# Half-height matmul operands outside the scores made full-height in a fused attention and mixer kernel

## The chip, the cores and the metric

The kernel runs on one core of a Trainium2 chip. The metric is the device time of one execution in microseconds. TensorE is PE in the rows, its weight loads PEld, VectorE DVE, ScalarE ACT, GpSimd POOL, and SP issues the DMAs.

## The reference

Causal attention of 4 batches x 12 heads (448 positions, 64 wide), then two MLP-mixer blocks on the [4, 448, 768] result. All is float32 or wider; the weights come in as doubles.

```python
attn = softmax(mask(q @ k.T / 8)); x = (attn @ v) as [4, 448, 768]
u = x + (relu(x.T @ w_tok1) @ w_tok2).T          # 448 -> 256 -> 448
x2 = u + relu(u @ w_ch1) @ w_ch2                 # 768 -> 1536 -> 768
g, v = split(relu(x2 @ w_in))                    # 512 each
v_n = (v - mean) / sqrt(var + 1e-6)
v_s = w_spatial @ v_n + b_spatial                # over the 448 positions
out = (g * v_s) @ w_out
```

## The kernel before

Every matrix product runs on operands that are split into two parts, hi and lo, and is the sum of hi x hi, hi x lo and lo x hi: three matmuls where one would do. The 448 positions are cut into chunks of 64, 128, 128 and 128, so that the causal mask wastes little. The first chunk has only 64 rows, half the height of the 128 x 128 array, and what the kernel does with those 64 rows is what the change is about. There are five places.

The scores (`scores`, line 190) multiply over the 64 channels of a head, one head on the upper half of the partitions and one on the lower half. The change leaves them as they are.

The other four:

- **The value's first chunk** (`weighted`, line 269, V0 and V1 in the order for the two heads of a pair): 64 keys of head j stand on the half `r` of the partitions, and the product with the transposed probabilities takes that half alone, twice (hi and lo of the probabilities). Then lines 271, 273 and 275 multiply the other three key chunks at full height. All accumulate into one PSUM bank.
- **The transposes** (`transposed`, line 247, T0 in the order): for the first key chunk of both heads there are four transposes, one for each query chunk. The query chunk of 64 rows is a half-height transpose, 64 x 64; the other three are 128 x 128.
- **The token mixing** (`token_mix`, lines 329 to 331 and 121 to 123, tile `psm<-xs,wt`): the hidden layer of a group of three pairs of heads is made in two parts, h0 and h1. Each is eleven matmuls: line 329, then line 330, which takes the low weights of the first chunk on the upper half of the partitions alone, then nine at full height. There are eight groups, so line 330 runs 16 times.
- **The spatial product** of the second block (`spatial`, lines 623 to 625, tile `psp`): the same shape again, with line 624 the half-height one; four column blocks for each of four batches, so 16 times.

The attention and the token mixing run interleaved, in an order that is written out by hand (`ORDER`): for each pair of heads a list of steps S (scores and softmax of a query chunk), T (transposes and their split), V, m (token mixing), q and v (splits of the inputs), each lagging the pair by up to three. Each engine takes its instructions in that order. There are 24 pairs. After that come the channel mixing (four batches x 12 weight chunks), the gated unit's input, the spatial products and the output projection.

POOL splits v into hi (line 76) and lo (line 82, tile `vhl`), splits the low part of q and k (line 82, tile `qk`), and multiplies the probabilities by the reciprocal sums (line 226). DVE does the row maxima (line 205), the low parts out of PSUM (lines 82 and 89), the sums into `U` (lines 280 and 364) and, in spare places, the narrowing of the doubles (lines 106, 108 and 110, tile `w`). ACT does the exponentials (line 217) and the high parts (line 74, and line 351 for `hid`).

Of the kernel before, what the change touches and what calls it, by code (L numbers as in the profile page):

```python
# [8 lines left out]
F32 = mybir.dt.float32  # L9
# [19 lines left out]
# The engines' order of work in the attention and token mixing, for one pair of heads: each name  # L29
# stands for the next step of a unit, each ' for one pair earlier.  # L30
# [9 lines left out]
def mixer_kernel(ctx: ExitStack, tc: tile.TileContext, qkv, wtok, w12, winu, winv, wsp, wout, bsp, out):  # L40
    """Every matrix product runs as float32r products of operands that are split
    exactly into two parts of 12 significant bits: hi * hi + hi * lo + lo * hi.

    On-chip memory is one pool of tagged slots which the phases share:
      U0-3     x^T, u^T, x2^T of each batch, later the gate
      G0-16    6 KB each: attention's and the token mixing's tiles, the 12 weight
               chunks of the channel mixing and the split of the running one, the
               input weights and normalised values of the gated unit
      X0-5     split operands of 448 columns, both parts
      h0-1     split hidden activations and gated values  # L50
      p0-1     narrow probabilities, unsplit gated values
      dbl0-1   float64 weights on their way in
    """
# [41 lines left out]
    def fetch(x):  # L95
        """Rows of doubles to SBUF as 32-bit words, the low word of each first."""
        n = 2 * x.shape[-1]
        t = slot(f"dbl{turn('dbl', 2)}", [2 * 2 * DM], U32, "dbl")
        nc.sync.dma_start(t[:, :n], x.bitcast(U32))
        return t[:, :n].rearrange("p (c t) -> p c t", t=2)  # L100

    def narrow_steps(w, d):
        """Doubles as words to float32: sign and top exponent bit, then the next 27 bits, then the top 3 of the low word."""
        w = w.bitcast(U32)
        lo, hi = d[:, :, 0], d[:, :, 1]
        nc.vector.tensor_scalar(w, hi, 3, 0x3FFFFFFF, op0=ALU.logical_shift_left, op1=ALU.bitwise_and)
        yield
        nc.vector.scalar_tensor_tensor(w, hi, 0xC0000000, w, op0=ALU.bitwise_and, op1=ALU.bitwise_or)  # L108
        yield
        nc.vector.scalar_tensor_tensor(w, lo, 29, w, op0=ALU.logical_shift_right, op1=ALU.bitwise_or)  # L110
        yield
# [5 lines left out]
    def mm3(ps, terms, first=True, last=True):  # L117
        """ps += sum of a.T @ b over terms of split operands (ah, al, bh, bl)."""
        n = len(terms)
        for i, (ah, al, bh, bl) in enumerate(terms):  # L120
            nc.tensor.matmul(ps, ah, bh, start=(first and i == 0), stop=False)  # L121
            nc.tensor.matmul(ps, ah, bl, start=False, stop=False)  # L122
            nc.tensor.matmul(ps, al, bh, start=False, stop=(last and i == n - 1))  # L123

# [15 lines left out]
    stage = [slot(f"G{i}", [3 * S], F32, f"stage{i}") for i in range(2)]  # L140
# [9 lines left out]
    def split_qk(n):  # L150
        """Splits q and k of a pair of heads."""
        st = stage[n % 2][:, : 2 * S]
        h, l = (slot(f"X{3 * (n % 2) + i}", [2 * S], F32R, "qk") for i in range(2))
        operands[n] = [h, l]
        parts = [slice(i * S, i * S + S) for i in range(2)]
        for c in parts:
            hi_part(h[:, c], st[:, c])
            yield
        for c in parts:
            lo_part(l[:, c], st[:, c], h[:, c], "dve" if n == 0 else "pool")  # L160
            if c is parts[1]:
                load_qk(n + 2)
            yield

    def split_v(n):
        """Splits v of a pair of heads, its parts side by side."""
        st = stage[n % 2][:, 2 * S :]
        vhl = slot(f"X{3 * (n % 2) + 2}", [7, 128], F32R, "vhl")
        v = st.rearrange("p (c d) -> p c d", d=64)
        hi_part(vhl[:, :, 0:64], v, "pool")  # L170
        yield
        lo_part(vhl[:, :, 64:128], v, vhl[:, :, 0:64], "pool")
        operands[n].append(vhl)
        load_v(n + 2)
        yield

    def scores(n, i):
        """Normalised probabilities of query chunk i; head 0 has its key chunks in reverse."""
# [20 lines left out]
        if i < 2 and "small" not in p:  # L199
            p["small"] = slot(f"p{n % 2}", [512], F32, "P10")  # L200
            p[1] = p["small"][:, 0:384].rearrange("p (j w) -> p j w", j=2)
            p[0] = p["small"][:, 384:512].rearrange("p (j w) -> p j w", j=2)
# [28 lines left out]
    def transposed(n, which, j):  # L231
        """Probabilities with keys on partitions, split: 0 for both heads' first key chunk, a and b of head j for the others."""
        P = [probs[n][i].rearrange("p j w -> p (j w)") for i in range(4)]

        def block(i, c):
            W, (k0, k1) = CHUNKS[i][1], CHUNKS[c]
            return P[i][:, slice(W + k0, W + k1) if j else slice(W - k1, W - k0)]

        if which == "0":
            blocks = [(q0, q1 - q0, P[i][: q1 - q0, q1 - 64 : q1 + 64]) for i, (q0, q1) in enumerate(CHUNKS)]  # L240
        elif which == "a":
            blocks = [(128 * (i - 1), 128, block(i, 1)) for i in (1, 2, 3)]
        else:
            blocks = [(128 * (i - 2), 128, block(i, 2)) for i in (2, 3)] + [(256, 128, block(3, 3))]
        ps = bank(SB + turn("t", TB), "pst")
        for o, M, src in blocks:
            nc.tensor.transpose(ps[:, o : o + M], src, ident[:M, :M])  # L247
        yield
        if which == "0":
            t = slot(f"h{n % 2}", [2, S], F32R, "T0")  # L250
        else:
            if (n, j) not in PT:
                PT[n, j] = slot(f"G{4 + j}", [4, 384], F32R, "Tab")
            t = PT[n, j][:, 0:2] if which == "a" else PT[n, j][:, 2:4]
        h, l = t[:, 0, :], t[:, 1, :]
        ps = ps[:, : h.shape[-1]]
        hi_part(h, ps)
        yield
        lo_part(l, ps, h)
        PT[n, which, j] = (h, l)  # L260
        yield

    def weighted(n, j):
        """x^T of head j: V^T P^T for V's two parts on the two halves of the partitions, then their sum."""
# [3 lines left out]
        for k in range(2):  # L268
            nc.tensor.matmul(ps[:, :S], vhl[r, 0, :], PT[n, "0", 0][k][r, :], start=(k == 0), stop=False)
        for k in range(2):  # L270
            nc.tensor.matmul(ps[:, 64:S], vhl[:, 1 + 3 * j, :], PT[n, "a", j][k], start=False, stop=False)  # L271
        for k in range(2):
            nc.tensor.matmul(ps[:, 192:S], vhl[:, 2 + 3 * j, :], PT[n, "b", j][k][:, 0:256], start=False, stop=False)
        for k in range(2):
            nc.tensor.matmul(ps[:, 320:S], vhl[:, 3 + 3 * j, :], PT[n, "b", j][k][:, 256:384], start=False, stop=(k == 1))
# [8 lines left out]
    WT = {}  # L284

    def load_tok():
        """Token weights, as steps."""
# [22 lines left out]
    def token_mix(n, m):  # L310
        """Part 3 * (n % 3) + m of 9 of the token mixing of a batch's three pairs of heads."""
# [6 lines left out]
        for s in todo:  # L318
# [7 lines left out]
            elif s[0] == "h":  # L326
# [3 lines left out]
                nc.tensor.matmul(p[:, :384], w[1][0:64, 0], x[0][0][0:64], start=False, stop=False)  # L330
# [42 lines left out]
    def split_slot(i, f):  # L373
        """For the split of part i of chunk f."""
        return f"G{15 + i}" if f % 2 == 0 else f"G{i}"

    def get_w12(f, nxt=True):
        """The weights' chunk f as float32, the next ones on their way."""
# [44 lines left out]
    WI = {}  # L423

    def get_win(i):
        """Input weights, part i of 4, split."""
# [92 lines left out]
    # the gate's columns, then the values, normalised over channels  # L519
# [14 lines left out]
    def value(lhs, key):  # L534
# [13 lines left out]
        # one Newton step of 1/sqrt(a)  # L548
# [44 lines left out]
    # spatial products, gating and the output weights  # L593
# [6 lines left out]
    def normed(b):  # L600
# [6 lines left out]
        ns.append((t[:, 0, :], t[o, 0, :]))  # L607
# [8 lines left out]
        return ns, o  # L616

    def spatial(b, ns, o):
        gs = []
        for f in range(NG):  # L620
            c = slice(128 * f, 128 * f + 128)
            ps = bank(turn("g", 4), "psp")[:, :S]
            nc.tensor.matmul(ps, ns[0][0][:, c], wsps[0][0], start=True, stop=False)
            nc.tensor.matmul(ps, ns[0][1][:, c], wsps[1][0][o], start=False, stop=False)
# [10 lines left out]
    def project(b, gs):  # L635
# [4 lines left out]
        # two row blocks wait for the last gated chunk together  # L640
# [20 lines left out]
    for b in range(B):  # L661
        gs = spatial(b, *ns)
# [6 lines left out]
def _layout(inputs):  # L669
    import numpy as np  # L670

    def chunked(a):
        """[448, n] -> [128, 4, n]: 64 rows (in both halves), then three times 128."""
# [7 lines left out]
    qkv = np.empty((B, NP, 128, 3 * S), q.dtype)  # L681
# [4 lines left out]
    qkv[..., 2 * S : 2 * S + D] = v[:, :, :64].reshape(B, NP, 128, D)  # L686
    qkv[..., 2 * S + D :] = (
# [45 lines left out]
```

## Time and profile before

| what | value |
|---|---|
| time, median of 3 runs | 898.4 us (896.5 to 899.64) |
| span of the profiled execution | 895.9 us |
| PE busy | 854.0 us (95%) |
| DVE, ACT, POOL busy | 510.1, 406.1, 423.8 us |
| attention and token mixing | from 0 to about 300 us |
| channel mixing, gated unit | about 300 to 785 us |
| spatial products and projection | 785 to 896 us |

The profiled execution has no time of its own beside the span from its first to its last instruction; the median of the runs is 2.5 us above it. Matmuls are pipelined, so their durations overlap, and the busy time of PE says little about how close it is to its limit. What one matmul takes from the next is read from the chain of work that ended last, where each piece counts only from the end of the piece before it.

### The profile page before, as it was taken

The numbers are of one execution on the slowest core, as the hardware profiler recorded it, in microseconds if no ns is written. First come the engines' busy times: TensorE is split into PE (matmuls) and PEld (weight loads), VectorE is DVE, ScalarE is ACT, GpSimd is POOL, SyncE is SP. The second block draws the span as 40 slices with busy tenths as digits, with TensorE's granted clock in tenths as the row PEclk, the third lists the DMA queues.
The fourth block names the chain that finished last, engine by engine and source line by source line (L and its number), as shares of the span: only waits on it lengthen the run. The fifth ranks groups of instructions, "written<-read, shape, count | busy, mean of one in ns | idle before, by whom it ended". The sixth has DMA issues, their size and how long they took to land.

```text
span 895.9 us, 12396 instructions
## 1 busy us (share of the span) xinstructions
PE 854.0 (95%) x4492; PEld 724.2 (81%) x4492; DVE 510.1 (57%) x1252; ACT 406.1 (45%) x958; POOL 423.8 (47%) x418
## 2 busy tenths in 40 slices
PE   4989999999999998999999999999989999999998
PEld 3667677677777887899999999999978888777877
DVE  5896998998889999240005000733382355364342
ACT  5686788788887322242224223433323133322111
POOL 5775776777776164545555544566640000322010
PEclk9988999999999999999999999999999999999999
DMA  5341323241210455200000000021101000001111
GB/s 191 116 150 53 133 65 124 67 137 48 76 31 11 142 212 209 74 0 1 1 1 1 1 1 1 15 99 70 64 20 58 1 1 1 1 20 42 62 62 62
DMA packets 13597, 54.24 MB, mean 61 GB/s; under 512 B 1504, under 2 KB 7776, under 8 KB 11104
## 3 DMA queue, kind: packets, MB, share of 16 engines
q1 hardware_dynamic: 13536, 53.45, 17.3%
q8 instruction: 35, 0.57, 0.3%
q14 instruction: 26, 0.21, 0.1%
HBM read 47.94 MB, written 5.51 MB: 60 GB/s over the span
## 4 chain that ended last, share of the span: by engine, by line
PE 73%; DVE 18%; ACT 5%; DMA 2%; issue 1%; POOL 0%; SPq 0%; ACTq 0%; DVEq 0%
PE acc L122 6%; PE acc L123 6%; PE acc L121 6%; PE ps L121 5%; PE ps L122 5%; PE ps L123 5%; PE pst L247 4%; PE pss L190 4%; DVE w L110 3%; DVE w L108 2%; PE psg L123 2%; PE psg L121 2%; PE psg L122 2%; PE pso L271 2%; ACT P L217 2%; PE psv L122 2%
## 5 line engine op out<-in xcount | busy, mean ns | idle before, releaser
L82 POOL TENSOR_TENSOR whl<-w,whl 128x768 fp32r<-128x768 f32 (+1 forms) x100 | 185.9, 1860 | 176.1 <-ACT whl L74 176.1
L89 DVE SCALAR_TENSOR_TENSOR hid<-ps,hid 128x448 fp32r<-128x448 f32 x48 | 29.7, 620 | 184.3 <-ACT hid L92 184.3
L74 ACT CAST whl<-w 128x768 fp32r<-128x768 f32 (+1 forms) x100 | 80.6, 806 | 114.1 <-PE acc L123 107.1
L226 POOL TENSOR_SCALAR P<-P,rs 128x320 f32<-128x320 f32 (+1 forms) x192 | 97.9, 523 | 66.9 <-DVE rs L223 57.3
L122 PE MATMUL acc<-hid,whl 128*128 128x448 f32 x288 | 106.3, 369 | 9.0 <-DVE hid L89 9.0
L123 PE MATMUL acc<-hid,whl 128*128 128x448 f32 x288 | 105.8, 367 | 0.0
L121 PE MATMUL acc<-hid,whl 128*128 128x448 f32 x288 | 105.8, 367 | 0.0
L121 PE MATMUL ps<-uhl,whl 128*128 128x448 f32 x288 | 105.4, 366 | 0.0
L122 PE MATMUL ps<-uhl,whl 128*128 128x448 f32 x288 | 105.4, 366 | 0.0
L123 PE MATMUL ps<-uhl,whl 128*128 128x448 f32 x288 | 105.2, 365 | 0.0
L217 ACT ACTIVATE P<-P,nm 128x320 f32<-128x320 f32 (+1 forms) x192 | 95.8, 503 | 6.6 <-DVE nm L205 6.5
L247 PE MATMUL pst<-ident,P 128*128 128x128 f32 (+1 forms) x384 | 72.9, 300 | 9.5 <-DVE rs L223 3.6
L190 PE MATMUL pss<-qk 64*128 64x448 f32 (+3 forms) x576 | 68.6, 344 | 9.6 <-ACT qk L74 5.5
L92 ACT ACTIVATE hid<-ps 128x448 fp32r<-128x448 f32 x48 | 26.1, 544 | 111.5 <-PE ps L123 111.4
L205 DVE CUSTOM_DVE_ANT_0 P<-pss,mask 128x320 f32<-128x320 f32 (+1 forms) x192 | 75.8, 410 | 1.2 <-PE pst L247 0.5
L190 PEld LDWEIGHTS pss<-qk 64*128 64x128 f32 (+1 forms) x576 | 43.7, 191 | 30.2 <-issue 15.5
L122 PEld LDWEIGHTS acc<-hid,whl 128*128 128x128 f32 x288 | 54.5, 189 | 15.2 <-DVE hid L89 10.9
L247 PEld LDWEIGHTS pst<-ident,P 128*128 128x128 f32 (+1 forms) x384 | 43.4, 148 | 25.9 <-issue 15.4
L121 PEld LDWEIGHTS acc<-hid,whl 128*128 128x128 f32 x288 | 54.5, 189 | 4.4
L123 PEld LDWEIGHTS acc<-hid,whl 128*128 128x128 f32 x288 | 54.5, 189 | 4.3
L123 PEld LDWEIGHTS ps<-uhl,whl 128*128 128x128 f32 x288 | 54.1, 188 | 4.3
L121 PEld LDWEIGHTS ps<-uhl,whl 128*128 128x128 f32 x288 | 54.1, 188 | 4.2
(144 smaller groups left out, 1872.1 us busy)
## 6 DMA issues: line engine op xcount, KB each, us to landing
dbl<-in_w SPq DMA_DIRECT2D x12, 1536.0 KB, 6.5
stage<-in_qkv SPq DMA_DIRECT2D x24, 448.0 KB, 3.3
stage<-in_qkv SPq DMA_DIRECT2D x24, 224.0 KB, 2.8
out_t<-out SPq DMA_DIRECT2D x24, 224.0 KB, 1.9
dbl<-in_winu SPq DMA_DIRECT2D x2, 1536.0 KB, 6.4
dbl<-in_winv SPq DMA_DIRECT2D x2, 1536.0 KB, 7.0
dbl<-in_wout SPq DMA_DIRECT2D x2, 1536.0 KB, 6.2
dbl<-in_wtok SPq DMA_DIRECT2D x1, 1024.0 KB, 7.3
```

What stands on the lines that cost most here:

```text
L74: nc.scalar.copy(hi, x)
L82: e.tensor_tensor(lo, x, hi.bitcast(F32), op=ALU.subtract)
L89: nc.vector.scalar_tensor_tensor(lo, x, 0.0, hi.bitcast(F32), op0=ALU.max, op1=ALU.subtract)
L110: nc.vector.scalar_tensor_tensor(w, lo, 29, w, op0=ALU.logical_shift_right, op1=ALU.bitwise_or)
L121: nc.tensor.matmul(ps, ah, bh, start=(first and i == 0), stop=False)
L122: nc.tensor.matmul(ps, ah, bl, start=False, stop=False)
L123: nc.tensor.matmul(ps, al, bh, start=False, stop=(last and i == n - 1))
L190: nc.tensor.matmul(pss[j][:M, :W], a[r, q0:q1], c[r, ks[j]], start=(k == 0), stop=(k == 2))
L205: nc.vector.tensor_tensor_reduce(out=P[:M, j, :], in0=pss[j][:M, :W], in1=mask[:M, S - 128 : S - 128 + W] if j == 0 or M == 64 else mask[: ...
L217: nc.scalar.activation(P[:M, j, :], P[:M, j, :], AF.Exp, bias=nm[:M, j : j + 1], scale=-1.0, accum_out=sums[:M, j : j + 1])
L226: nc.gpsimd.tensor_scalar(P[:M, j, :], P[:M, j, :], rs[:M, j : j + 1], 1.0, op0=ALU.mult, op1=ALU.mult)
L247: nc.tensor.transpose(ps[:, o : o + M], src, ident[:M, :M])
```

## The change

The half-height operands of the four places become full-height ones, so that outside the scores each matmul has 128 rows.

- Value: the split of v has 8 blocks of 64 columns instead of 7. Blocks 0 and 1 are the first key chunks of head 0 and head 1, each with zeros on the other head's half of the partitions. The zeros come in from memory with v: its load grows from 448 to 512 columns (224 to 256 KB a pair), and so do POOL's two splits of it.
- Transposes: the first query chunk is transposed as 128 x 128. Its rows 64 to 127 are zeros, set once by two memsets on POOL at the start, for which the two small tiles of probabilities are now allocated once and kept. The 64 columns too many are written over by the next transpose.
- Token mixing and spatial product: line 330 and line 624 take the low weights on both halves of the partitions, where the other operand holds hi on one half and lo on the other. So lo x lo comes in as well, in the same instruction.

No matmul is added or taken away, and none changes its place on its engine. The diff also takes out comments and docstrings; that part is left out here.

```diff
+    small = [slot(f"p{i}", [512], F32, f"P10{i}") for i in range(2)]
+    for t in small:
+        nc.gpsimd.memset(t[64:128, 384:512], 0.0)
-    stage = [slot(f"G{i}", [3 * S], F32, f"stage{i}") for i in range(2)]
+    stage = [slot(f"G{i}", [2 * S + 512], F32, f"stage{i}") for i in range(2)]
...
-        vhl = slot(f"X{3 * (n % 2) + 2}", [7, 128], F32R, "vhl")
+        vhl = slot(f"X{3 * (n % 2) + 2}", [8, 128], F32R, "vhl")
...
-            p["small"] = slot(f"p{n % 2}", [512], F32, "P10")
+            p["small"] = small[n % 2]
...
-            blocks = [(q0, q1 - q0, P[i][: q1 - q0, q1 - 64 : q1 + 64]) for i, (q0, q1) in enumerate(CHUNKS)]
+            blocks = [(q0, 128, P[i][:, q1 - 64 : q1 + 64]) for i, (q0, q1) in enumerate(CHUNKS)]
...
-            nc.tensor.matmul(ps[:, :S], vhl[r, 0, :], PT[n, "0", 0][k][r, :], start=(k == 0), stop=False)
+            nc.tensor.matmul(ps[:, :S], vhl[:, j, :], PT[n, "0", 0][k], start=(k == 0), stop=False)
...
-                nc.tensor.matmul(p[:, :384], w[1][0:64, 0], x[0][0][0:64], start=False, stop=False)
+                nc.tensor.matmul(p[:, :384], w[1][:, 0], x[0][0], start=False, stop=False)
...
-            nc.tensor.matmul(ps, ns[0][1][:, c], wsps[1][0][o], start=False, stop=False)
+            nc.tensor.matmul(ps, ns[0][:, c], wsps[1][0], start=False, stop=False)
...
-    qkv = np.empty((B, NP, 128, 3 * S), q.dtype)
+    qkv = np.zeros((B, NP, 128, 2 * S + 512), q.dtype)
...
-    qkv[..., 2 * S : 2 * S + D] = v[:, :, :64].reshape(B, NP, 128, D)
-    qkv[..., 2 * S + D :] = (
+    for j in range(2):
+        qkv[..., 64 * j : 64 * j + 64, 2 * S + D * j : 2 * S + D * j + D] = v[:, j::2, :64]
+    qkv[..., 2 * S + 2 * D :] = (
```

## Rows read from the trace of the kernel before

**Rows 1.** The page: span, and each engine's busy time (share) and instructions.
```profile
span 895.9 us, 12396 instructions
PE 854.0 (95%) x4492; PEld 724.2 (81%) x4492; DVE 510.1 (57%) x1252; ACT 406.1 (45%) x958; POOL 423.8 (47%) x418
```

**Rows 2.** The page: the chain that ended last, its shares by engine.
```profile
PE 73%; DVE 18%; ACT 5%; DMA 2%; issue 1%; POOL 0%; SPq 0%; ACTq 0%; DVEq 0%
```

**Rows 3.** That chain in order of time, one group: start us, us, what.
```profile
172.51 0.35 PE pst L247 x3
...
173.37 0.43 PE pso L269 x2
...
175.11 0.17 PE psm L329
175.28 0.36 PE psm L330
175.65 0.37 PE psm L121
...
177.44 0.68 PE pst L247 x4
...
187.10 0.52 ACT U L278
```

**Rows 4.** The chain again, the last value products: start us, us, what.
```profile
281.80 0.60 PE pso L269 x2
282.39 0.55 PE pso L271 x2
...
289.52 1.90 DVE w L110
```

**Rows 5.** The chain again, the spatial products of the first batch.
```profile
791.71 0.21 PE psp L123
...
792.12 0.40 PE psp L624
792.52 0.40 PE psp L121
...
801.47 1.01 DVE ghl L82
```

**Rows 6.** Half-height matmuls: line, shape, count, duration in ns (min/median/max), starts.
```profile
L330 PE MATMUL psm<-xs,wt x16: 436/442/686, 71.1 to 302.8; 64*128 64x384 f32 x16
L624 PE MATMUL psp<-hw,nsh x16: 463/468/469, 785.2 to 875.2; 64*128 64x448 f32 x16
```

**Rows 7.** DVE's timeline at h0 and h1 of one group, idle time before.
```profile
178.00 0.56 DVE L89 SCALAR_TENSOR_TENSOR hid<-psm,hid 128x384 fp32r<-128x384 f32 x1 [0.49 <-ACT hid L351]
...
181.76 0.56 DVE L89 SCALAR_TENSOR_TENSOR hid<-psm,hid 128x384 fp32r<-128x384 f32 x1 [1.61 <-ACT hid L351]
```

**Rows 8.** POOL's splits of v: count, duration in ns (min/median/max), starts.
```profile
L76 POOL TENSOR_SCALAR vhl<-stage x24: 555/564/572, 7.3 to 275.2; 128x448 fp32r<-128x448 f32 x24
L82 POOL TENSOR_TENSOR vhl<-stage,vhl x24: 1127/1149/1461, 24.4 to 286.0; 128x448 fp32r<-128x448 f32 x24
```

**Rows 9.** Waits between 80 and 260 us: total us, times, longest.
```profile
POOL P L226 <- DVE rs L223: 35.2, 17, 3.5
```

**Rows 10.** The chain again, at the start.
```profile
2.58 7.32 DMA dbl<-in_wtok
```

**Rows 11.** Busy us (and instructions) in two stretches; behind POOL the granted clock.
```profile
50.00:80.00 30.00, 27.71 (x153) 20.96 (x149) 21.62 (x78) 19.37 (x58) 20.61 (x31) 0.77 0.23 70
80.00:110.00 30.00, 28.43 (x193) 21.35 (x191) 29.15 (x100) 24.73 (x74) 19.98 (x31) 1.00 0.31 102
```

**Rows 12.** PE's timeline: waits for DVE in two groups, idle time before.
```profile
57.55 0.55 PE L247 MATMUL pst<-ident,P 128*128 128x128 f32 x3 [0.70 <-DVE Tab L82]
...
60.43 0.52 PE L247 MATMUL pst<-ident,P 128*128 128x128 f32 x3 [1.04 <-DVE rs L223]
...
99.01 0.55 PE L325 MATMUL psm<-ident,U 128*128 128x128 f32 x3 [1.06 <-DVE U L364]
```

More of the change, by code (lines that the diff above doesn't have):

```diff
@@ L268, in weighted @@
         for k in range(2):
-            nc.tensor.matmul(ps[:, :S], vhl[r, 0, :], PT[n, "0", 0][k][r, :], start=(k == 0), stop=False)
+            nc.tensor.matmul(ps[:, :S], vhl[:, j, :], PT[n, "0", 0][k], start=(k == 0), stop=False)
         for k in range(2):
-            nc.tensor.matmul(ps[:, 64:S], vhl[:, 1 + 3 * j, :], PT[n, "a", j][k], start=False, stop=False)
+            nc.tensor.matmul(ps[:, 64:S], vhl[:, 2 + 3 * j, :], PT[n, "a", j][k], start=False, stop=False)
         for k in range(2):
-            nc.tensor.matmul(ps[:, 192:S], vhl[:, 2 + 3 * j, :], PT[n, "b", j][k][:, 0:256], start=False, stop=False)
+            nc.tensor.matmul(ps[:, 192:S], vhl[:, 3 + 3 * j, :], PT[n, "b", j][k][:, 0:256], start=False, stop=False)
         for k in range(2):
-            nc.tensor.matmul(ps[:, 320:S], vhl[:, 3 + 3 * j, :], PT[n, "b", j][k][:, 256:384], start=False, stop=(k == 1))
+            nc.tensor.matmul(ps[:, 320:S], vhl[:, 4 + 3 * j, :], PT[n, "b", j][k][:, 256:384], start=False, stop=(k == 1))
         yield
@@ L606, in normed @@
         split(t[o, 0, :], t[lo, 0, :], x[o])
-        ns.append((t[:, 0, :], t[o, 0, :]))
+        ns.append(t[:, 0, :])
         ts = [t[:, 1, :], t[:, 2, :]]
@@ L615, in normed, with spatial @@
             ns.append((ts[2 * c - 2], ts[2 * c - 1]))
-        return ns, o
-    def spatial(b, ns, o):
+        return ns
+    def spatial(b, ns):
         gs = []
@@ L622, in spatial @@
             ps = bank(turn("g", 4), "psp")[:, :S]
-            nc.tensor.matmul(ps, ns[0][0][:, c], wsps[0][0], start=True, stop=False)
-            nc.tensor.matmul(ps, ns[0][1][:, c], wsps[1][0][o], start=False, stop=False)
+            nc.tensor.matmul(ps, ns[0][:, c], wsps[0][0], start=True, stop=False)
+            nc.tensor.matmul(ps, ns[0][:, c], wsps[1][0], start=False, stop=False)
             mm3(ps, [(ns[i][0][:, c], ns[i][1][:, c], wsps[0][i], wsps[1][i]) for i in (1, 2, 3)], first=False)
@@ L661, in mixer_kernel @@
     for b in range(B):
-        gs = spatial(b, *ns)
+        gs = spatial(b, ns)
         if b + 1 < B:
```

## The prediction

> **What bounds the kernel now.** I read the page first, for the span and who is busy: the span is 895.9 us and PE is busy 95% of it [rows 1]. Overlapping matmuls make that share useless as a limit, so I went to the chain that ended last. It gives PE 73%, DVE 18% and ACT 5% [rows 2]. That is the first thing to see: time taken off PE is worth its full price in three quarters of the span and nothing in the rest, so each edit has to be placed before it is priced.
>
> Then I read the chain in order of time. In the attention it repeats for each group of three pairs. A stretch of PE alone holds two value products, h0, a T0, h1 and two more value products; the larger part of one, from 172.51 to where ACT takes over at 187.10, is shown [rows 3]. Then comes a stretch about as long in which DVE, ACT and short PE pieces alternate. Within the PE stretch the reader should look at the pieces beside a half-height matmul. Line 329 (128 rows, 384 columns) takes 0.17 us. Line 330, with 64 rows and as many columns, takes 0.36, and the next matmul, back at 128 rows, takes 0.37 [rows 3]. So the time goes with the change of height and not with the work: about 0.19 us to get into half height and 0.20 to get out. The spatial products show the same: 0.40 and 0.40 about line 624, where a matmul of that width at full height takes 0.21 [rows 5].
>
> **The change part by part.**
>
> *Token mixing.* Each h step falls from 0.36 + 0.37 to 2 x 0.17, a gain of 0.38 to 0.39 [rows 3]. Line 330 runs 16 times [rows 6]. Fourteen of these stand in PE stretches of the chain; the last two, of the last group, start after 289.52, where the chain runs through DVE's narrowing of weights [rows 4], and gain nothing. 14 x 0.38 = 5.3 us.
>
> *Transposes.* A T0 of four takes 0.68 us, because its first transpose is half-height between full-height neighbours. Three full-height ones take 0.35, so four take 0.47: 0.21 gained each [rows 3]. There are 24. By the chain 11 stand in PE stretches (one between h0 and h1 of each of seven groups, two in the first pairs, two among the last), the other 13 where DVE ends the wait. 11 x 0.21 = 2.3 us.
>
> *Value products.* Here the edit looks largest (96 matmuls, four a pair) and I expect least. 44 of the 48 come straight after scores, which are half-height too, so line 269 needs no switch: 0.43 for its two matmuls [rows 3], 0.21 each, as a full-height one of that width [rows 5]. The switch to full height falls on line 271 instead, 0.55 for two where 2 x 0.17 would do [rows 4]. After the change it falls on the first line 269. Moved, not removed: 0, and from the difference of entry and exit price (0.01 to 0.03 us) at most 1.3 us either way for the 44. Only the last four follow full-height work. The two on the chain, one of which is shown, take 0.60 and 0.55 [rows 4] where 0.42 and 0.35 would do: 0.38 each, 0.8 us. The other two come after DVE has taken the chain: 0.
>
> The Trainium skill (TensorEngine Tiling (Array Packing), Key Properties) says that different tiles can execute weight loads and matmuls in parallel. That speaks against making line 269 full-height: were its two matmuls run beside each other or beside the scores, the change would cost 48 x 0.21 = 10 us. The trace shows no such overlap here, 0.43 for the two, which use the same half.
>
> *Spatial products.* 16 times 0.40 + 0.40 against 2 x 0.21, a gain of 0.38: 6.1 us [rows 5]. Behind a batch's last column block, ACT's and DVE's chain to the projection (it ends with the 1.01 on `ghl`) starts when PE is through with the block, so it moves with it. A block takes PE 2.2 us instead of 2.6 then (eleven matmuls of 0.2), and DVE, which has three operations for it and waits for PE between blocks, keeps up.
>
> *At half clock.* Two T0s, the first h0 and the first spatial block stand where matmuls take nearly twice as long; their gains count about twice. An estimate from the prices above: 2 x 0.21 + 2 x 0.38 = 1.2, of which I take 0.6, since a stretch at half clock may end elsewhere.
>
> *What the change adds.* POOL's two splits of v grow by 512/448: 0.08 and 0.16 us a pair [rows 8], 24 x 0.24 = 5.8 us of POOL time. Below it costs nothing: POOL waits 35.2 us between 80 and 260 us for the reciprocal sums alone [rows 9], over twice what all pairs add. Above, all 5.8 would show, if each split were late for a transpose or held DVE's access. Queued behind the splits are the multiplications by the sums, which T0, Ta and Tb read; PE's waits in the steady groups end on DVE, not on POOL. Nearer to the lower end: 0.5. The two memsets stand before POOL's first split, which waits for q and k from memory anyway: 0. Two larger loads of v are queued on SP ahead of the token weights, whose 7.32 us stand on the chain at the start [rows 10]; 64 KB more of some 3.3 MB under way is 2%, 0.15, rounded up to 0.2.
>
> *Can the others follow?* In such a PE stretch DVE waits 0.49 us at h0 and 1.61 at h1 [rows 7]. PE will be 0.38 earlier at h0 and 0.97 at h1; both waits shrink but neither closes, so DVE doesn't become the bound inside the stretch. Next late after it is DVE, with rather little idle time left.
>
> Sum: 5.3 + 2.3 + 0.8 + 6.1 + 0.6 - 0.5 - 0.2 = 14.4 us off the span, 895.9 to 881.5; with the 2.5 us by which the median stands above it, 884.0.
>
> **The rivals.**
>
> *The clock helps.* Between 50 and 80 us the granted clock is 0.77 on average, some 14 us at 1.2 instead of 2.4 GHz, and PE gets through 153 matmuls; in the next 30 us it is 1.00 and 193 [rows 11]. That is (193 - 153) / 193 x 30 = 6.2 us. If the changed mix of matmuls avoids that, it is 884.0 - 6.2 = 878. For it: the stretch holds scores, value products and transposes, much of it half-height, and ends in the full-height token mixing. Against: transposes, which the change only touches at 1 in 16, make up much of it.
>
> *The clock hurts (the other side).* PE had waited 0.70 and 1.04 us for DVE before it lost its clock [rows 12]. Where DVE is the bound, a faster PE waits longer, by up to two T0s, 0.4 us a group. If that drops the clock in further groups, each costs 6.2 us: one makes 890, two 896, and from the third the kernel is slower, 903. Against: in the next group it waits 1.06 us for DVE [rows 12] and the clock stays at 1.00 [rows 11]. The Trainium skill (TensorE: Matmul & The Clock Gate, HAM oscillation) states the mechanism, idle gaps between bursts of matmuls bringing the lower clock back; the trace agrees in one place [rows 11, 12].
>
> *DVE or POOL takes the attention's gain.* If the alternating stretches grow by what the PE stretches lose, 5.3 + 2.3 goes and the spatial products' part stays: 892.
>
> *The change doesn't do it.* If the 0.2 us belonged to something else than the height (the operand's address, the accumulation), lines 330 and 624 would stay at 0.36 and 0.40, and only the costs would be left: 899. Against: each of the four places shows it on entry and exit, and no neighbour does.
>
> **How the numbers follow.** Chances: forecast 0.60 (own range 880 to 888), clock helps 0.16, attention's gain lost 0.11, clock hurts once 0.05, twice 0.03, three times or more 0.03, nothing happens 0.02. The time is that of the likeliest, 884. The range reaches down to the better clock with the price bounds under it, 875, and up to the lost gain, 892, and leaves out 0.08 by the cases and as much again by their spread. About 0.3%, 2.7 us, is what a measurement of this kernel can tell from no change. Faster: 0.60 + 0.16 + 0.11 + 0.05 = 0.92. Same (twice, nothing): 0.05. Slower: 0.03.
>
> **What would show it.** In the changed kernel's chain, lines 329 to 123 of an h step should all take 0.17 to 0.18 us, T0 some 0.47 for four, the spatial matmuls all about 0.20. The first line 269 after scores should take about 0.4 and line 271's two 0.35, together as before. DVE's waits at h0 and h1 should be about 0.1 and 1.0. PE's waits for DVE at the end of a group should grow by at most 0.4. I am wrong if the granted clock shows other stretches at half, if POOL's splits end waits of PE, or if the alternating stretches lengthen.

## The result and the profile after

| | before | changed |
|---|---|---|
| median of the runs (range) | 898.2 us (896.5 to 899.64, 4 runs) | 885.14 us (882.48 to 890.95, 4 runs) |
| span of the profiled execution | 895.9 us | 883.8 us |
| ratio to before, 95% interval | | 0.9865 [0.983, 0.99] |

The changed kernel is 1.35% faster. It was run twice more beside the experiments: 884.13 us (6 runs, 0.984 [0.9799, 0.9881]) and 885.13 us (6 runs, 0.9862 [0.9819, 0.9906]). Ratios here and below leave out slow executions, those more than 1.5% above the fastest of their kernel, while the medians include them.

The page after, span and busy time, which answers to [rows 1]:

```profile
span 883.8 us, 12419 instructions
PE 828.5 (94%) x4492; PEld 726.7 (82%) x4492; DVE 515.8 (58%) x1252; ACT 405.3 (46%) x958; POOL 428.8 (49%) x420
```

PE has lost 25.5 us of busy time with the same 4492 matmuls, twice what the span lost: durations of matmuls overlap, so a busy share is no price. POOL has gained 5.0 us with two instructions more (the memsets) and DVE 5.7 with none. Line numbers are about four higher than before (330 is 334 now, 269 is 273, 247 is 251, 624 is 628, 190 is 194).

PE's timeline at one h0 (start us, us, what), which answers to [rows 3], before and then changed:

```profile
175.21 0.44 PE L330 MATMUL psm<-xs,wt 64*128 64x384 f32 x1
175.58 0.44 PE L121 MATMUL psm<-xs,wt 128*128 128x384 f32 x1
175.86 0.34 PE L122 MATMUL psm<-xs,wt 128*128 128x384 f32 x1
```

```profile
174.02 0.42 PE L333 MATMUL psm<-xs,wt 128*128 128x384 f32 x1
174.27 0.34 PE L334 MATMUL psm<-xs,wt 128*128 128x384 f32 x1
174.45 0.34 PE L121 MATMUL psm<-xs,wt 128*128 128x384 f32 x1
174.63 0.33 PE L122 MATMUL psm<-xs,wt 128*128 128x384 f32 x1
```

In this view the durations of neighbours overlap; what a matmul costs is the step from its start to the next start. Before, line 330 to line 121 is 0.37 us and line 121 to 122 is 0.28; changed, both steps are 0.18. From line 329 (it starts at 174.87 before) to the first line 122 the whole falls from 0.99 to 0.61, the 0.38 that was priced.

The chain after, spatial products of the first batch, which answers to [rows 5]:

```profile
787.31 0.21 PE psp L627
787.51 0.20 PE psp L628
787.72 0.20 PE psp L121
...
793.85 1.01 DVE ghl L82
```

All matmuls take 0.20 to 0.21 there, and DVE's piece on `ghl` behind them is still 1.01.

Where the 12.1 us of the two spans went, from starts in PE's timeline:

| event | before | changed | gained so far |
|---|---|---|---|
| sixth pair's 64x64 scores | 75.90 | 72.30 | 3.6 |
| last pair's 64x64 scores | 278.31 | 270.86 | 7.45 |
| first matmul of the channel mixing into `acc` | 312.11 | 304.37 | 7.74 |
| first spatial product | 784.85 | 778.79 | 6.06 |
| end | 895.9 | 883.8 | 12.1 |

The spatial stage gives 6.0 us. The attention gives 7.7, of which 1.7 is lost again in the channel mixing and the gated unit, which the change doesn't touch. These are two profiles only: in the other two of the changed kernel the first `acc` matmul stands at 302.93 and 305.99, 9.2 and 6.1 us ahead of before.

### The profile page after: what moved, and what is told of

Its sections match the earlier page's. It is cut to its first block, busy times and chain, and to the rows that moved or that the text cites. A ratio compares the mean times of both kernels' runs of the same rounds, so it can differ in the third digit from the quotient of the medians.

```text
span 883.8 us, 12419 instructions
## 1 busy us (share of the span) xinstructions
PE 828.5 (94%) x4492; PEld 726.7 (82%) x4492; DVE 515.8 (58%) x1252; ACT 405.3 (46%) x958; POOL 428.8 (49%) x420
## 4 chain that ended last, share of the span: by engine, by line
PE 56%; DVE 10%; ACT 1%; DMA 1%; issue 1%; ACTq 0%; DVEq 0%
PE acc L122 6%; PE acc L123 6%; PE acc L121 6%; PE ps L123 6%; PE ps L122 5%; PE ps L121 5%; DVE w L110 2%; PE psg L121 2%; PE psg L123 2%; PE psg L122 2%; PE psv L122 2%; PE psv L123 2%; PE psv L121 2%; PE pso L122 2%; PE pso L123 2%; PE pso L121 2%
## 5 line engine op out<-in xcount | busy, mean ns | idle before, releaser
L122 PE MATMUL acc<-hid,whl 128*128 128x448 f32 x288 | 107.4, 373 | 8.3 <-DVE hid L89 8.3
L123 PE MATMUL acc<-hid,whl 128*128 128x448 f32 x288 | 106.9, 371 | 0.0
L121 PE MATMUL acc<-hid,whl 128*128 128x448 f32 x288 | 106.9, 371 | 0.0
L123 PE MATMUL ps<-uhl,whl 128*128 128x448 f32 x288 | 105.3, 366 | 0.0
L122 PE MATMUL ps<-uhl,whl 128*128 128x448 f32 x288 | 105.3, 365 | 0.0
L251 PE MATMUL pst<-ident,P 128*128 128x128 f32 x384 | 66.7, 289 | 20.1 <-DVE rs L227 10.7
L251 PEld LDWEIGHTS pst<-ident,P 128*128 128x128 f32 x384 | 42.7, 144 | 30.2 <-issue 14.9
L122 PEld LDWEIGHTS acc<-hid,whl 128*128 128x128 f32 x288 | 55.3, 192 | 14.3 <-DVE hid L89 9.8
L121 PEld LDWEIGHTS acc<-hid,whl 128*128 128x128 f32 x288 | 55.2, 192 | 4.5
L123 PEld LDWEIGHTS acc<-hid,whl 128*128 128x128 f32 x288 | 55.3, 192 | 4.4
```

## The experiments

My theory: a change of height costs 0.2 us each way on PE, so line 330 and line 624 give most of the gain, the transposes some, and the value part about nothing. The rivals: the gain comes from the clock at the start, or the value part matters, by its padding on POOL and DVE or by its height on PE.

Single executions of any of these kernels scatter by several us (the one with the value part alone from 890.91 to 901.97), and in the profiles the stretches in which PE runs at 1.2 GHz come at different places: the kernel with the spatial edit alone runs the program of before up to its spatial products, and over its first 80 us the granted clock was 0.98 against 0.91. So beside the time each experiment is read from one group of three pairs in the steady part of the attention, from the 64x64 scores of one pair to those three pairs later, where the granted clock is 1.00 throughout. The columns are the stretch, its length, the busy time (and count) of PE, PEld, DVE, ACT and POOL, the granted clock, the DMA share and GB/s. Before, and then changed:

```profile
178.05:211.46 33.41, 32.36 (x222) 24.57 (x221) 29.88 (x106) 28.09 (x85) 25.05 (x39) 1.00 0.34 110
```

```profile
173.42:205.90 32.48, 30.57 (x223) 25.22 (x222) 30.63 (x106) 27.92 (x85) 25.39 (x38) 1.00 0.37 117
```

The group is 0.93 us shorter, with DVE busy 0.75 us longer. Its length repeats: 32.48 in all three profiles of the changed kernel, and 33.36 (175.55 to 208.91) in the kernel with the spatial edit alone, whose attention is that of before. So differences of 0.05 are scatter.

### Low weights alone, with and without the spatial product

The kernel before, with the one line of the token mixing and the one of the spatial product:

```diff
-                nc.tensor.matmul(p[:, :384], w[1][0:64, 0], x[0][0][0:64], start=False, stop=False)
+                nc.tensor.matmul(p[:, :384], w[1][:, 0], x[0][0], start=False, stop=False)
...
-            nc.tensor.matmul(ps, ns[0][1][:, c], wsps[1][0][o], start=False, stop=False)
+            nc.tensor.matmul(ps, ns[0][0][:, c], wsps[1][0], start=False, stop=False)
```

> The kernel before with the low weights over both halves alone (token mixing and spatial product; lo x lo comes in as in the changed kernel). Theory (a change of height costs PE 0.19 to 0.20 us each way, paid where the chain runs through PE): 14 x 0.38 + 16 x 0.38 = 11.4 us off, 886.8, with the spatial stage alone shorter by 6.1. Rival (in the attention DVE takes back what PE gives): only the spatial part stays, 892.

Measured: 887.61 us (6 runs), 0.9899 [0.9855, 0.9942]. The window of the group:

```profile
176.03:208.62 32.59, 31.56 (x221) 24.52 (x220) 29.90 (x106) 28.13 (x85) 25.05 (x39) 1.00 0.35 113
```

It is 0.82 shorter than before for two h steps, priced at 2 x 0.38 = 0.76. DVE's timeline shows what is left of its waits:

```profile
175.98 0.56 DVE L89 SCALAR_TENSOR_TENSOR hid<-psm,hid 128x384 fp32r<-128x384 f32 x1
...
179.38 0.56 DVE L89 SCALAR_TENSOR_TENSOR hid<-psm,hid 128x384 fp32r<-128x384 f32 x1 [1.17 <-ACT hid L351]
```

0.49 and 1.61 [rows 7] have become none and 1.17: DVE loses its idle time at h0 and doesn't hold PE up.

The second diff line alone:

> The kernel before with the spatial low weights alone over both halves. Theory: 6.1 us off, 892, all of it between 785 us and the end; the attention as before. Rival (DVE's chain behind each batch takes a part back): 3 to 4 off, with longer waits of PE for the gated chunks.

Measured: 892.19 us (12 runs), 0.996 [0.9927, 0.9993]. From the first spatial product (782.81) to the end (888.1) it takes 105.3 us, against 111.05 before and 105.0 in the changed kernel. The whole time moved by 0.6 to 6.6 us by the interval, which holds the 5.8 between them. Not every profile shows this gain. The first 12 us of the stage, in the changed kernel and in its first repetition:

```profile
778.79:790.79 12.00, 12.00 (x51) 11.00 (x52) 8.68 (x19) 3.69 (x8) 2.09 (x2) 0.86 0.00 0
776.25:788.25 12.00, 11.51 (x56) 10.35 (x56) 10.11 (x20) 4.09 (x8) 3.63 (x3) 1.00 0.00 0
```

With the clock at 0.86 there, the stage takes 111.0 to 111.5 us in the five profiles with the half-height line and 104.8 to 105.7 in six with the full-height one, 5.9 less on average. Three more with the full-height line, both repetitions of the changed kernel and the one with line 269 half-height below, have the clock at 1.00 and take 103.5 to 103.6. What kept the clock up in these is not shown.

### Transposes alone

```diff
+    small = [slot(f"p{i}", [512], F32, f"P10{i}") for i in range(2)]
+    for t in small:
+        nc.gpsimd.memset(t[64:128, 384:512], 0.0)
...
-            p["small"] = slot(f"p{n % 2}", [512], F32, "P10")
+            p["small"] = small[n % 2]
...
-            blocks = [(q0, q1 - q0, P[i][: q1 - q0, q1 - 64 : q1 + 64]) for i, (q0, q1) in enumerate(CHUNKS)]
+            blocks = [(q0, 128, P[i][:, q1 - 64 : q1 + 64]) for i, (q0, q1) in enumerate(CHUNKS)]
```

> The kernel before with the full transposes alone. Theory: 0.21 to 0.25 us where the chain runs through PE, 11 times: 2.3 to 2.8 us off, 895.4, seen as a group shorter by 0.25 in its A pair (10.86 to 10.6) and not in B and C. Rival (all 24 pay): 5 to 6 off, 892.5.

Measured: 899.82 us (12 runs), 0.9962 [0.9921, 1.0003]; the time alone says little. The window of the group, and the chain over one T0 and the h0 behind it:

```profile
178.63:211.81 33.18, 31.68 (x223) 24.76 (x222) 29.87 (x105) 27.89 (x85) 24.78 (x39) 1.00 0.34 110
```

```profile
178.26 0.44 PE pst L251 x4
178.70 0.29 PE pss L194 x6
178.99 0.48 PE pst L251 x3
179.47 0.17 PE psm L333
179.65 0.37 PE psm L334
180.02 0.37 PE psm L121
180.39 0.17 PE psm L122
```

T0's four take 0.44 instead of 0.68 [rows 3], and the half-height line 334, left alone here, still takes 0.37 + 0.37. The group is 0.23 shorter. There are three T0s in a group, so only one of them pays, the one in the PE stretch, as priced (0.21).

### The value part alone, and the change without it

The value part is the padded load, 8 blocks instead of 7 in POOL's splits, and line 269 at full height. First the kernel before with it, then the changed kernel with these lines taken back (run twice; the changed kernel itself was repeated twice too, the second time on the same chip as the second of these). The packing of v and the block numbers of the other value products follow the new width:

```diff
-    stage = [slot(f"G{i}", [3 * S], F32, f"stage{i}") for i in range(2)]
+    stage = [slot(f"G{i}", [2 * S + 512], F32, f"stage{i}") for i in range(2)]
...
-        vhl = slot(f"X{3 * (n % 2) + 2}", [7, 128], F32R, "vhl")
+        vhl = slot(f"X{3 * (n % 2) + 2}", [8, 128], F32R, "vhl")
...
-            nc.tensor.matmul(ps[:, :S], vhl[r, 0, :], PT[n, "0", 0][k][r, :], start=(k == 0), stop=False)
+            nc.tensor.matmul(ps[:, :S], vhl[:, j, :], PT[n, "0", 0][k], start=(k == 0), stop=False)
```

> The kernel before with the padded, full-height value chunk alone. Theory (padding costs, height is neutral on PE): 899 to 902. Rival (it brings the clock up earlier): 893 to 896, with the clock up before 40 us.

> The changed kernel with the value's first chunk as before (half height, 7 blocks, load and splits of 448 columns). Theory (the padded value costs DVE and POOL time in the attention and delays the start, and gains nothing on PE): 2 to 4 us faster than the changed kernel, 881 to 883, first narrowing of the token weights back at about 9.9 us, DVE-bound groups 0.2 us shorter. Rival (full-height value products bring the clock up earlier, 35.7 us against 44.7, and shorten the half-clock stretch near 62 us): slower than the changed kernel, 887 to 889, with the clock up at 44 us or later.

> The changed kernel once more, for its spread: single runs of all these kernels scatter by 4 to 6 us, and the median of the changed kernel rests on four. If the padding costs what the steady groups show (0.16 us in one of three pairs, some 1.3 us): 883 to 886, about 1.3 above the kernel without the value part (882.9). If padding costs what the kernel with line 269 at half height shows beside that (889.5 against 882.9): 888 or more.

> The changed kernel without the value part, again. Theory (padding costs some 2.8 us by POOL and DVE, the full height of line 269 gives back some 1.5 in the groups and 2 or more by a shorter stretch at half clock at the start, so that the value part is worth nothing or a little less): within 2 us of the changed kernel, on either side. Rival (the value part costs 2 us or more): 882 or less beside 884.

> The changed kernel, on the same chip as the two kernels below, to compare with them alone: 884 to 885 as in both earlier measurements.

Measured: the value part alone 897.17 us (12 runs), 0.9987 [0.9955, 1.0019]; without it 882.93 us (0.9842 [0.9803, 0.9881]) and 887.12 us (0.9859 [0.981, 0.9908]); the changed kernel repeated 884.13 and 885.13 us. The windows of the group with the value part alone, and without it:

```profile
176.49:209.97 33.48, 32.09 (x223) 25.11 (x222) 30.13 (x106) 28.11 (x85) 25.60 (x39) 1.00 0.35 114
```

```profile
170.25:202.61 32.36, 30.86 (x223) 24.69 (x222) 30.07 (x106) 27.92 (x85) 24.78 (x39) 1.00 0.34 114
```

The value part costs a group 0.12 (32.48 - 32.36) on the changed kernel, about 1 us over the eight groups; the 0.07 on the kernel before is hardly more than the scatter. The times don't resolve that: the two medians without it lie on either side of the changed kernel's.

### Padding without height, height taken back, and the load without the splits

Is that small sum two small terms or two large ones? The padded load and splits, with line 269 still half-height, on the kernel before and on the changed one:

```diff
-            nc.tensor.matmul(ps[:, :S], vhl[:, j, :], PT[n, "0", 0][k], start=(k == 0), stop=False)
+            nc.tensor.matmul(ps[:, :S], vhl[r, j, :], PT[n, "0", 0][k][r, :], start=(k == 0), stop=False)
```

> The kernel before with v loaded and split as 512 columns with the zeros, and line 269 at half height as before: the cost of the padding by itself. Theory (0.16 us in one of three pairs by POOL's longer splits): 1.3 us more, 899.4. Rival 1 (padding costs 6 us, as the two kernels with line 269 at half height differ): 904. Rival 2 (no cost): 898. Beside the kernel with the value alone (897.2) it tells what the height of line 269 does: neutral if both are within 1 us, worth several us by the clock if this one is 901 or more.

> The changed kernel with line 269's matmuls on the half of the partitions again, while the load, the padding and the splits stay at 512 columns. If the padding alone is the cost and the height of line 269 is neutral: as the changed kernel, 885. If the height of line 269 is what brings the clock up earlier: 889 or more, with the clock as in the kernel before.

Measured: the padding alone 900.67 us (12 runs), 1.0034 [1.0004, 1.0063], slower than before. The changed kernel with line 269 half-height 889.45 us (12 runs), 0.9909 [0.9874, 0.9944]. The windows of the group, in this order:

```profile
182.21:216.00 33.79, 32.37 (x223) 24.58 (x222) 30.20 (x106) 28.11 (x85) 25.61 (x39) 1.00 0.35 112
```

```profile
178.76:211.50 32.74, 30.87 (x223) 24.68 (x222) 30.70 (x106) 27.88 (x85) 25.32 (x39) 1.00 0.36 116
```

The padding costs 0.38 a group (33.79 - 33.41), and the height gives back 0.31 on the kernel before (33.79 - 33.48) and 0.26 on the changed one (32.74 - 32.48). Two terms of a size, then, that nearly cancel. Whole runs put more on the height than eight groups would (2.1 to 2.5 us): 0.9909 with line 269 half-height against 0.984 to 0.9865 for the changed kernel, and 1.0034 against 0.9987 on the kernel before, 4 to 6 us. The intervals overlap, so how much of that is real, and how much of it the clock's, stays open.

Which part of the padding costs? The kernel before with v's load widened to 512 columns, 64 of zeros at its end, while POOL splits 448:

```diff
-    stage = [slot(f"G{i}", [3 * S], F32, f"stage{i}") for i in range(2)]
+    stage = [slot(f"G{i}", [2 * S + 512], F32, f"stage{i}") for i in range(2)]
...
-        st = stage[n % 2][:, 2 * S :]
+        st = stage[n % 2][:, 2 * S : 3 * S]
```

> The kernel before with v's load widened to 512 columns (64 of zeros at its end), while POOL still splits 448; every matmul as before. It tells which part of the padding makes a steady group of three pairs longer (33.79 us with the padded load and splits, 33.41 before, from 64x64 scores to 64x64 scores three pairs on). If the longer splits do it, by slowing DVE beside them: the group is 33.35 to 33.45, DVE's narrowing (128x384, the operation of 867 ns before and 930 with padded splits) stays at 860 to 875 ns, the time 896 to 900. If the larger transfer does it: the group is 33.7 to 33.8, the narrowing 920 or more, the time 899 to 902.

Measured: 898.81 us (8 runs), 0.9994 [0.9955, 1.0033]. The window of its group:

```profile
179.30:212.73 33.43, 32.38 (x223) 24.59 (x222) 29.87 (x106) 28.11 (x85) 25.05 (x39) 1.00 0.34 113
```

33.43 against 33.41: the larger load costs nothing there, and the splits cost it all. How they do shows in two operations of DVE that stand beside POOL's work. The first is the narrowing of line 110, which reads both operands from SBUF. Its group by line and shape (count, busy us, mean ns, idle time) over some ten pairs of steady attention, before and with the padded splits:

```profile
L110 DVE SCALAR_TENSOR_TENSOR w<-dbl,w 128x384 uint32<-128x384 uint32 x10 | 8.7, 867 | 0.0
```

```profile
L110 DVE SCALAR_TENSOR_TENSOR w<-dbl,w 128x384 uint32<-128x384 uint32 x10 | 9.3, 930 | 0.0
```

It becomes 63 ns longer; with the wide load and the short splits it is 870 ns. An operation of the same kind that reads one operand from PSUM (`hid`, line 89) stays at 557. The Trainium skill (SBUF — State Buffer, SBUF: two separate sides) says of a DVE operation with two SBUF inputs and a GpSimd one that reads SBUF that the first holds the shared ports for its whole instruction and "the other fully blocks". The trace agrees: in both profiles each of the nine narrowings that start in this stretch ends 0.40 to 0.42 us behind the end of a POOL operation that was under way when it started, seven times a multiplication by the sums (line 226) and twice the lo split of v.

In a pair whose end DVE sets, what DVE loses comes out in full. The second pair of the group, before and with the padded splits:

```profile
188.90:198.86 9.96, 9.81 (x69) 7.57 (x68) 9.86 (x35) 8.69 (x28) 8.58 (x14) 1.00 0.68 229
```

```profile
193.06:203.21 10.15, 9.81 (x69) 7.56 (x68) 10.05 (x35) 8.69 (x28) 8.78 (x14) 1.00 0.66 228
```

PE is busy 9.81 in both, DVE 0.19 longer, the pair 0.19 longer. That is half of the group's 0.38; the other half falls in the third pair (12.59 to 12.78, from the starts of its scores at 198.87 and 203.22 to the ends of the two windows), in which there is no narrowing. What both pairs have is the second operation, line 221, which adds a constant to the two sums of each row, beside POOL's lo split of v. From the timelines of DVE and POOL, before and with the padded splits:

```profile
189.94 0.59 DVE L221 TENSOR_SCALAR rs<-sums 128x2 f32<-128x2 f32 x1
199.24 0.95 DVE L221 TENSOR_SCALAR rs<-sums 128x2 f32<-128x2 f32 x1
189.05 1.46 POOL L82 TENSOR_TENSOR vhl<-stage,vhl 128x448 fp32r<-128x448 f32 x1
199.01 1.15 POOL L82 TENSOR_TENSOR vhl<-stage,vhl 128x448 fp32r<-128x448 f32 x1
```

```profile
194.17 0.72 DVE L221 TENSOR_SCALAR rs<-sums 128x2 f32<-128x2 f32 x1
203.59 1.12 DVE L221 TENSOR_SCALAR rs<-sums 128x2 f32<-128x2 f32 x1
193.26 1.59 POOL L82 TENSOR_TENSOR vhl<-stage,vhl 128x512 fp32r<-128x512 f32 x1
203.42 1.27 POOL L82 TENSOR_TENSOR vhl<-stage,vhl 128x512 fp32r<-128x512 f32 x1
```

Elsewhere line 221 mostly takes 0.15 us. Here it ends 0.02 to 0.03 us behind the end of the split each time (190.53 and 190.51 in the first), and so do all 60 of its executions in these two profiles that take over 0.25 us, behind one POOL operation or another. The longer split keeps it 0.13 longer in the second pair, where the narrowing ahead of it adds 0.06, and 0.18 longer in the third: 0.37 of the 0.38. PE's waits for the sums behind it grow as much, from 0.15 to 0.34 and from 0.62 to 0.80. Line 221 reads one tensor, so the case of two inputs doesn't cover it; by which rule POOL holds it no run shows.

### Full height only at the ends

If the value part helped by the clock at the start, and cost by its padding in the steady groups, then it should be made full-height for the first pairs alone (and the last two, whose products follow full-height work):

```diff
+def blocks_of(n):
+    return 8 if n < 4 or n >= 22 else 7
...
+            if nb == 8:
+                nc.tensor.matmul(ps[:, :S], vhl[:, j, :], PT[n, "0", 0][k], start=(k == 0), stop=False)
+            else:
+                nc.tensor.matmul(ps[:, :S], vhl[r, 0, :], PT[n, "0", 0][k][r, :], start=(k == 0), stop=False)
```

> Full-height, padded value chunk for the first four pairs and the last two alone (blocks 0 and 1 with zeros, loads and splits of 512 columns); the 18 between as in the kernel before. Theory (the height pays at the start, where it shortens the time at half clock, and the padding costs in the groups between): 0 to 3 us faster than both, 880 to 883, with groups of 33.2, 33.2 and 32.3 us as without the value part, and the clock up by 36 us. Rival (the height does nothing for the clock): as without the value part, first stretches at half clock of 47 us or more in the first 80.

Measured: 886.55 us (6 runs), 0.988 [0.9833, 0.9928], no better than the changed kernel beside it (885.13). Its steady group is 32.34 us (171.81 to 204.15), as without the value part, but in the profiled execution a stretch with PE at 1.2 GHz for part of the time came near the end of the attention:

```profile
255.00:275.00 20.00, 18.52 (x104) 15.36 (x103) 14.65 (x47) 13.39 (x39) 11.15 (x16) 0.74 0.05 14
```

A clock of 0.74 over 20 us costs PE up to 5.2 us (0.26 x 20), more than the padding of 18 pairs costs (six groups at 0.38 make 2.3). Over the first 80 us the clock was 0.94, as in one of the two profiles without the value part and below the other (1.00), so that full height in the first pairs helps the clock isn't shown. No version here beats the changed kernel beyond doubt.

## Why the prediction was right

**The time.** 884.0 was forecast, 885.14 measured, inside the likeliest case's own range. The sum of 14.4 us off the span was 2.3 too much; the added 2.5 us for what lies outside the span was 1.8 (885.61 us for the profiled execution with a span of 883.8).

**Token mixing, priced 5.3.** Held: 0.82 a group against 0.76. The price belongs to the height: in the steady stretch the half-height line stays at 0.37 + 0.37 in the kernel that changes the transposes alone, and a group loses the priced time where only the heights of the low weights are changed. The Trainium skill (TensorEngine Tiling (Array Packing), Key Properties) states that "Changing tiling mode (not just tile) drains the TensorE"; the rows put some 0.2 us on it in each direction, and it goes when the mode no longer changes.

**Transposes, priced 2.3.** Held in the steady groups: 0.23 for three T0s against 0.21. Placing each edit before pricing it was what mattered: 24 T0s at 0.21 would have been 5 us.

**Spatial products, priced 6.1.** Held: 6.0 in the first profile, 5.9 on average where the stage has its stretch at half clock, as before. The two repetitions of the changed kernel gained 7.6, since that stretch didn't come.

**Value products, 0 for the 44 behind scores.** The net was near, the step not quite. (That each of the four places pays on entry and exit, as the prediction says against its last rival, isn't so here by its own account: 44 of these have no entry.) "Moved, not removed" predicted that height gives nothing there; it gives 0.26 to 0.31 a group. PE's timeline over one V0 shows where, with the padding in both kernels, half-height and then full-height:

```profile
174.13 0.87 PE L190 MATMUL pss<-qk 64*128 64x448 f32 x6
175.08 0.64 PE L269 MATMUL pso<-T,vhl 64*128 64x448 f32 x2
175.65 0.61 PE L271 MATMUL pso<-Tab,vhl 128*128 128x384 f32 x2
...
176.51 0.51 PE L247 MATMUL pst<-ident,P 128*128 128x128 f32 x3
```

```profile
168.61 0.88 PE L190 MATMUL pss<-qk 64*128 64x448 f32 x6
169.56 0.65 PE L269 MATMUL pso<-T,vhl 128*128 128x448 f32 x2
170.06 0.51 PE L271 MATMUL pso<-Tab,vhl 128*128 128x384 f32 x2
...
170.82 0.52 PE L247 MATMUL pst<-ident,P 128*128 128x128 f32 x3
```

Scores to line 269 is 0.95 in both, so the switch into full height costs nothing that shows at this place; line 269 to 271 falls from 0.57 to 0.50 and 271 to 273 and 275 follow, 2.38 to 2.21 for the whole. Line 269 starts a little behind the end of the scores, so a likely reading is that the switch fits into that wait; no run shows the wait apart from the switch. The 0.8 for the last pair's products didn't arrive: from the last 64x64 scores to the first `acc` matmul is 33.80 before and 33.51 now, but 33.53 without the value part and 33.82 with the value part alone (276.96 to 310.78), so the 0.3 there isn't its own.

**POOL, priced 0.5 between 0 and 5.8.** Mis-sized, and the step that failed: POOL's long waits for the reciprocal sums [rows 9] were taken as cover for longer splits. The cover doesn't matter, since the cost comes by DVE's operations beside POOL's, line 221 above all, which ends only when the split does. 0.38 a group over eight groups is 3.0, on the kernel before; whole runs with the padding alone were 0.04 to 0.63% slower than before, 0.4 to 5.7 us. "Held DVE's access" was named as the way to the upper end and given too little weight.

**DMA, priced 0.2.** Nothing in the steady groups. At the start single executions scatter by more than 0.2, so the term itself isn't told apart.

**Can the others follow.** The forecast was 0.1 and 1.0 for DVE's waits at h0 and h1; the trace shows none and 0.71. DVE is nearer to being the bound than forecast, but in the PE stretch it isn't yet.

**Clock.** Both clock rivals came about in part, and with them one of the prediction's own signs of being wrong, other stretches at half clock. The stretch of [rows 11] after:

```profile
50.00:80.00 30.00, 25.89 (x177) 20.92 (x178) 27.73 (x94) 22.80 (x69) 20.28 (x32) 0.94 0.23 76
80.00:110.00 30.00, 27.67 (x191) 22.58 (x189) 28.10 (x97) 22.81 (x69) 22.61 (x34) 0.94 0.37 124
```

The clock is 0.94 instead of 0.77 in the first, with 177 matmuls instead of 153, and 0.94 instead of 1.00 in the second, in which PE's wait for DVE at the end of a group has grown from 1.06 [rows 12] to 1.26. Two later stretches are lower as well (0.97 instead of 1.00 from 300 to 350 us, 0.91 instead of 0.96 from 640 to 680), which is where the 1.7 us in the untouched stages went: matmul by matmul the lead falls by 0.6 in the first, by 1.1 in the second and nowhere else in these stages. So 0.6 for "at half clock" was a term of several us in both directions that happened to cancel. POOL was priced 2.5 us too low, the 0.8 didn't arrive, and the height of line 269 gave some 2 that were priced at nothing, so that the sum came out as close as this is partly luck.

**What stays open.** Why these stretches come where they do. Over the first 80 us of the profiles the granted clock is 0.94 to 0.98 in the five executions with line 269 at full height in the first pairs; with it at half height it is 0.87 to 0.94 in seven, but 0.98 and 1.00 in two more. That is a tendency, not a cause: one of the last two, at 0.98, runs the program of before up to there. Whether the value part is worth its place stays open with it.

## What to carry to other kernels

Price a change of operand height by its entries and exits, some 0.4 us for a lone half-height matmul between full-height ones, and count only those that stand where PE alone sets the time. Where the other half of the partitions already held the other part of a split operand (lines 330 and 624), full height cost nothing that shows. If it has to be padded with zeros, price the padding on the engine that splits or copies it and, above all, on what the other engines do beside that: look for short operations there that end just behind the long one. Where single executions scatter by more than the effect, compare the length of one steady stretch at a granted clock of 1.00: there the parts (0.82 + 0.23 - 0.07) added up to the whole (0.93) within 0.1 us.

## What the runs showed of the hardware that was not expected

- A DVE operation on two columns (line 221), 0.15 us by itself, lasted until the POOL operation beside it ended, up to 0.95 us before. A POOL split 14% wider (448 to 512 columns) made that 1.12, while POOL itself had waits of 35.2 us to spare [rows 9].
- Executions of one program lie 1.5% apart (892.65 to 905.63 us with the load alone), and the granted clock falls below 1.00 in stages where the change touches nothing (0.91 from 640 to 680 us).
